# Psum copies of the w2-transpose products and of the last output products fixed to ScalarE, and three n3 stores moved to ScalarE's queue

## The chip, the cores and the metric

The kernel runs on one core of a Trainium2 chip, as one program. A core has TensorE (PE), VectorE (DVE), ScalarE (ACT), GpSimd (POOL) and SyncE (SP), each with its own instruction queue that is worked off in order, and they meet by semaphores. The metric is the device time of one execution in microseconds; the number given is the median of several runs.

## The reference

One block of a spectral transformer with adaptive norms, forward and backward, in bf16, with S = 2048 tokens, D = 1024 channels and F = 3584 hidden channels:

```python
mod = (_silu(c) @ w_mod).reshape(c.shape[0], 6, 1, -1)   # sa, ca, ga, sb, cb, gb
h = _layernorm(x) * (1 + ca) + sa
x = x + ga * A(h)          # A: rfft2 over (S, D), times w_r + 1j*w_i, irfft2
h = _layernorm(x) * (1 + cb) + sb
x = x + gb * B(h)          # B: layernorm, gelu(y @ w1 + b1) @ w2 + b2
...
out, vjp = jax.vjp(f, A_x, A_w_r, A_w_i, B_w1, B_b1, B_w2, B_b2, c, w_mod)
return (out, *vjp(grad_out))
```

The outputs are the forward result and the gradients of nine inputs. n3 below is the output of the third layer norm, the input of w1.

## The kernel before, in words

The program goes through five stages. First come the modulation rows and the first norm. The forward spectral mixer follows, with the 2D transform as matrix products: `spectral_core(True, ...)`, up to about 390 us. Beside its end PE computes the products "ph" = w2 transposed times the gated output gradient, and the stage ends in the z blocks, which make z = w1 n3 and the gelu with its derivative, interleaved with `bo_pass`, the second MLP product and the forward output (to about 500 us). The backward products through w1 follow, then the backward mixer with the norms' backward passes, beside which the gradients of w2 and of w1 are made as a list of pieces that fill PE.

Work on an engine stands in the order in which the tile scheduler put it when the program was built. `tc.high_priority()` and `tc.issue_after(...)` steer it; `nc.any` leaves it to the scheduler which of DVE and ACT does a copy.

The parts that the change and the prediction touch:

- **ph_part** (L832 to L847). For each of 28 blocks of 128 hidden channels and each of four quarters of the tokens, 8 matmuls of 128x512 (L839) fill a psum tile `pp`, of which there are four. A copy by `nc.any` (L845) puts it into `pho` or `phr` in SBUF; after the fourth quarter POOL stores the block to `d_ph`.
- **consume_fwd** (L884 to L904). For each quarter i of the tokens the inverse transform's output products `po` (L774, copies L779 and L781) are unfolded by additions on DVE (helper line L195), the result is stored by POOL (`d_A`), x is added, and two norms are applied. Statistics come from DVE (L493, L494, L503) and, for some rows, from ACT (L507, L510); the square root is ACT's L483; ACT applies the norm (L518). For the last quarter DVE applies the third norm. Line L904 stores n3 from SP to `d_n3`, 1024 KB at a time. The buffer from which it is stored (`ct`) is needed again for the unfolding of a later quarter. The two norms of a quarter go through the same scratch tile `mv`.
- **SP's queue** around there also holds the DMA transposes that load w2 transposed (L342 into `wt`), w1 and the reloads of `d_ph`. A store of n3 stands in line with these.
- **z_block** (L961 to L1002). For each group of four blocks: four products (L976), four ACT passes with the bias (L979), square (L983), two sigmoids (L987, L989), and on DVE L984, L990 and products (L195). `gt` are its tiles, `hhA`, `hhB`, `hhC` its results. In `bo_pass` PE sums the gradient of gb (L1049), and DVE brings the sum from psum to SBUF (L1052).
- **Backward**: `consume_bwd` (from L1474) unfolds, loads x again, applies the norm on ACT (L518) after the copy that is kept in `last_po`, multiplies, and calls the norm's backward (L1250, L1256, L1259). The pieces of the gradient of w1 run beside it: 16 matmuls (L1565) into a psum tile `gw1acc`, a copy by ACT (L1569) and a store. Psum tiles of `po` come from the same set as those of `gw1acc` for one copy in four.

Of the kernel before, what the change touches and what calls it, by code (L numbers as in the profile page):

```python
# [35 lines left out]
def kernel(  # L36
# [24 lines left out]
    nc = tc.nc  # L61
# [47 lines left out]
    d_n3 = dram.tile([S, D], BF16, name="d_n3")  # L109
# [16 lines left out]
    def chunk_rows(dt, i):  # L126
        return dt[4 * i * P:4 * (i + 1) * P, :].rearrange("(q p) d -> p q d", p=P)
# [400 lines left out]
    last_po = [None]  # L528
# [19 lines left out]
    def spectral_core(fwd, fb, sms, em, css, pt, evac_u, evac_c, evac_v, consume, o4tag, pfs=None, fill=lambda n: None, mid=lambda: None, beside=lambda n, r_in: None):  # L548
# [156 lines left out]
        for par in range(2):  # L705
            for m in range(4):
# [14 lines left out]
                if par == 0 and m > 0:  # L721
# [6 lines left out]
                    else:  # L728
                        cl = (CE, SE)[m - 2]
                        for h in range(2):  # L730
                            with tc.issue_after((ld_in if fwd else hh_in)[0].ins):
                                nc.sync.dma_start_transpose(out=gm[:, 2 * cl:2 * cl + 2, h * P:(h + 1) * P],
                                                            in_=d_E[:, v, 2 * cl + h, :])
# [22 lines left out]
        for i in range(4):  # L756
# [7 lines left out]
            for npp, (cl, ov4, c0) in enumerate((half if i % 2 == 0 else []) + [(cl, o4[:, cl], i * P) for cl in (CO, SO)]):  # L764
                if npp in (2, 4) and (fwd or (i, npp) != (0, 2)):
                    fill(1)
                for hh_ in range(2):
                    npo[0] += 1
                    po = ((ps_d, ps_s) if fwd else (ps_d, ps_s, ps_d, ps_f))[npo[0] % (2 if fwd else 4)]("po")
                    for d2 in range(2):  # L770
                        dc = 2 * hh_ + d2
                        for h in range(2):
                            gi = 2 * dc + h + (4 if (dc >= 2 and cl >= 2) else 0)
                            nc.tensor.matmul(po[:, d2 * 256:(d2 + 1) * 256], lhsT=Vs[cl][:, 2 * dc + h, c0:c0 + P],  # L774
                                             rhs=gm[:, gi, :], start=(h == 0), stop=(h == 1))
                    with tc.high_priority():
                        ov = ov4[:, hh_ * 512:(hh_ + 1) * 512]
                        if fwd or (cl, hh_) != (3, 0):
                            nc.any.tensor_copy(out=ov, in_=po[:])  # L779
                        else:  # L780
                            last_po[0] = nc.scalar.copy(out=ov, in_=po[:])  # L781
            if i % 2 == 0:
                tt(o4[:, 0:4:2, :], eb[:, 0:2, :], eb[:, 2:4, :], ALU.add)
                if fwd and i == 2:
# [49 lines left out]
    def ph_part(fc, js):  # L834
        ph2 = phs[fc % 4]
        for j in js:
# [5 lines left out]
            ov = ph2[:, :, q * P:(q + 1) * P]  # L842
            pv = pp[:, :].rearrange("p (i w) -> p i w", w=P)
            with tc.high_priority():
                nc.any.tensor_copy(out=ov, in_=pv)  # L845
        if js[-1] == 3:
            nc.gpsimd.dma_start(out=d_ph[fc * P:(fc + 1) * P, :], in_=ph2.rearrange("p i w -> p (i w)"))  # L847

# [35 lines left out]
    def consume_fwd(i, o4, tmp, tmp2, x4, eb):  # L884
# [14 lines left out]
        else:  # L899
            for q in range(4):  # L900
                t = 4 * i + q
                nc.vector.tensor_scalar(out=tmp[:, q, :], in0=tmp[:, q, :], scalar1=stats[:, 2, 0, t:t + 1],
                                        scalar2=stats[:, 2, 1, t:t + 1], op0=ALU.mult, op1=ALU.add)
        nc.sync.dma_start(out=chunk_rows(d_n3, i), in_=tmp)  # L904

    spectral_core(True, fbuf, (smA, smB), em1[:, 1], [css[:, 0], css[:, 1]], new_pair_temps(PXT[2:6]),
                  act_copy, act_copy, act_copy, consume_fwd, "fr")
# [789 lines left out]
```

## Time and profile before

| what | before |
|---|---|
| median of 3 runs | 1398.17 us (1397.17 to 1399.39) |
| profiled execution | 1398.61 us |
| its span, first to last instruction | 1396.8 us |
| busy share of PE / DVE / ACT / POOL | 97% / 76% / 55% / 25% |
| mean granted TensorE clock | 0.990 |
| copies of `pp` by ACT / DVE | 77 / 35 |
| copies of `po` by ACT / DVE | 43 / 21 |

The times that one reads in the trace are of the profiled execution, and start at its first instruction. Rows of the timeline give start, duration, engine, line, operation, output and inputs, the number of equal instructions in a row, and in brackets how long the engine stood idle before and what ended that. Rows that belong together overlap a little at their ends, so several in a row take less than their durations' sum. A windows row gives, for one stretch of time, the busy time of each engine (with the number of instructions), the granted clock of TensorE, the share of the DMA engines and GB/s. A DMA's time from issue to landing stands last in the rows on DMA issues.

### The profile page before, as it was taken

The numbers are of one execution on the slowest core, as the hardware profiler recorded it, in microseconds if no ns is written. First come the engines' busy times: TensorE is split into PE (matmuls) and PEld (weight loads), VectorE is DVE, ScalarE is ACT, GpSimd is POOL, SyncE is SP. The second block draws the span as 40 slices with busy tenths as digits, with TensorE's granted clock in tenths as the row PEclk, the third lists the DMA queues.
The fourth block names the chain that finished last, engine by engine and source line by source line (L and its number), as shares of the span: only waits on it lengthen the run. The fifth ranks groups of instructions, "written<-read, shape, count | busy, mean of one in ns | idle before, by whom it ended". The sixth has DMA issues, their size and how long they took to land.

```text
span 1396.8 us, 18464 instructions
## 1 busy us (share of the span) xinstructions
PE 1351.6 (97%) x6774; PEld 657.6 (47%) x6899; DVE 1063.7 (76%) x1471; ACT 767.6 (55%) x1090; POOL 347.8 (25%) x434
## 2 busy tenths in 40 slices
PE   4998999999999999999999999999999999999998
PEld 2545566444444444444444444444654555444444
DVE  4997889977888787787811388889888489976990
ACT  4875657657977766656503684445732454534311
POOL 5410533301212122122111011011444320332351
PEclk8999999999999999999999999999999999999999
DMA  9982755899787777697999979988679978899991
GB/s 318 289 237 57 202 143 189 259 273 357 241 246 247 229 248 239 202 275 247 244 319 219 220 185 272 306 275 231 216 221 259 222 205 200 218 232 239 292 344 64
DMA packets 360689, 331.12 MB, mean 237 GB/s; under 512 B 207962, under 2 KB 303088, under 8 KB 360470
## 3 DMA queue, kind: packets, MB, share of 16 engines
q1 hardware_dynamic: 319702, 204.96, 56.9%
q0 software_dynamic: 35136, 119.73, 25.0%
q10 hardware_dynamic: 5760, 5.25, 1.2%
q8 instruction: 54, 0.88, 0.3%
q14 instruction: 37, 0.30, 0.1%
HBM read 165.73 MB, written 114.87 MB: 201 GB/s over the span
## 4 chain that ended last, share of the span: by engine, by line
PE 72%; DVE 7%; DMA 3%; issue 1%; ACT 1%; ACTq 0%; DVEq 0%
PE pg L1130 14%; PE gw1acc L1565 13%; PE gw2acc L1302 13%; PE pz L976 13%; PE pbo L1030 13%; DVE ct L195 4%; PE pp L839 2%; PE po L774 1%; DVE st L493 1%; PE pcs L581 1%; DMA hhsA<-d_hh 1%; DMA w2sA<-in_B_w_dram 1%; DMA d_n<-ct 1%; PE acc3a L218 1%; PE pu L542 1%
## 5 line engine op out<-in xcount | busy, mean ns | idle before, releaser
L839 PE MATMUL pp<-gBoT,wt 128*128 128x512 bf16 x874 | 197.9, 383 | 4.1 <-ACT phr L845 2.9
L1130 PE MATMUL pg<-w1T,gzr 128*128 128x512 bf16 x877 | 194.3, 379 | 1.3 <-issue 0.5
L1565 PE MATMUL gw1acc<-gzh,n3n 128*128 128x512 bf16 x626 | 139.1, 379 | 3.6 <-DVE ct L779 2.8
L839 PEld LDWEIGHTS <-wt 128*128 128x128 bf16 x896 | 88.0, 98 | 108.2 <-issue 7.3
L1565 PEld LDWEIGHTS <-n3n 128*128 128x128 bf16 x896 | 87.4, 98 | 108.2 <-issue 4.4
L1130 PEld LDWEIGHTS <-gzr 128*128 128x128 bf16 x896 | 86.6, 98 | 108.4 <-issue 5.8
L976 PEld LDWEIGHTS <-w 128*128 128x128 bf16 x896 | 87.3, 98 | 106.8 <-issue 2.4
L976 PE MATMUL pz<-n3Tb,w 128*128 128x512 bf16 x437 | 98.4, 379 | 1.6 <-DVE w2sD L1052 0.9
L976 PE MATMUL pz<-n3Ta,w 128*128 128x512 bf16 x439 | 98.0, 379 | 0.4
L195 DVE TENSOR_TENSOR ct<-ct 128x2048 bf16<-128x2048 bf16 (+1 forms) x84 | 91.6, 1119 | 7.1 <-DMA d_n<-ct 4.7
L1030 PEld LDWEIGHTS <-hhA 128*128 128x128 bf16 x608 | 58.9, 98 | 72.7 <-issue 2.5
L1302 PE MATMUL gw2acc<-gB,hhsA 128*128 128x512 bf16 x405 | 91.7, 379 | 0.6
L1569 ACT CAST gwo<-gw1acc 128x512 bf16<-128x512 f32 x56 | 32.2, 581 | 108.3 <-PE gw1acc L1565 87.8
L979 ACT ACTIVATE gt<-pz,b_col 128x512 bf16<-128x512 f32 x112 | 72.9, 682 | 33.3 <-PE pz L976 33.0
L987 ACT ACTIVATE gt<-gt 128x2048 bf16<-128x2048 bf16 x28 | 53.5, 1911 | 64.3 <-DVE gt L195 64.3
L195 DVE TENSOR_TENSOR gt<-gt,gt 128x2048 bf16<-128x2048 bf16 x56 | 68.6, 1224 | 19.8 <-ACT gt L989 18.5
L1310 ACT CAST gwo<-gw2acc 128x512 bf16<-128x512 f32 x40 | 23.6, 590 | 85.8 <-PE gw2acc L1302 85.8
L1302 PEld LDWEIGHTS <-hhsA 128*128 128x128 bf16 x416 | 40.7, 98 | 47.2
L1565 PE MATMUL gw1acc<-gzu,n3n 128*128 128x512 bf16 x251 | 55.2, 379 | 0.3
L983 ACT ACTIVATE gt<-gt 128x2048 bf16<-128x2048 bf16 x28 | 53.5, 1909 | 2.3 <-DVE hhC L195 1.6
L989 ACT ACTIVATE gt<-gt 128x2048 bf16<-128x2048 bf16 x28 | 53.4, 1907 | 0.4
L1302 PE MATMUL gw2acc<-gB,otl 128*128 128x512 bf16 x218 | 49.2, 379 | 0.4 <-issue 0.2
(371 smaller groups left out, 2511.0 us busy)
## 6 DMA issues: line engine op xcount, KB each, us to landing
gzr<-d_gz SPq DMA_DIRECT2D x28, 512.0 KB
wblk<-in_w_mod_dram SPq DMA_DIRECT2D x12, 1024.0 KB
d_ph<-pho POOLq DMA_DIRECT2D x21, 512.0 KB, 5.6
out_dram<-otl POOLq DMA_DIRECT2D x40, 256.0 KB, 4.8
d_hh<-hhA POOLq DMA_DIRECT2D x19, 512.0 KB, 5.0
wrw<-in_w_mod_dram SPq DMA_DIRECT2D x32, 256.0 KB
w<-in_B_w_dram SPq DMA_DIRECT2D x7, 1024.0 KB
hhC<-d_ph SPq DMA_DIRECT2D x14, 512.0 KB
```

What stands on the lines that cost most here:

```text
L195: return nc.vector.tensor_tensor(out=out, in0=a, in1=b, op=op)
L839: last_pe[0] = nc.tensor.matmul(pp[:], lhsT=wt[:, fc % 4, cch, :], rhs=gBoT[j][:, cch, :], start=(cch == 0), stop=(cch == NDC - 1))
L976: last_pe[0] = nc.tensor.matmul(pz[:], lhsT=w1s[g][:, cch, k * P:(k + 1) * P], rhs=n3T[:, cch, :], start=(cch == 0), stop=(cch == NDC - 1))
L979: z_in = nc.scalar.activation(out=zb[:, k, :], in_=pz[:], func=ACT.Identity, bias=b1_col[:, fc:fc + 1], scale=1.0)
L983: nc.scalar.activation(out=av, in_=zb, func=ACT.Square)
L987: nc.scalar.activation(out=sg, in_=bv, func=ACT.Sigmoid, scale=2.0 * GK)
L989: nc.scalar.activation(out=bv, in_=bv, func=ACT.Sigmoid, scale=-2.0 * GK)
L1030: last_pe[0] = nc.tensor.matmul(pbs[i][:], lhsT=hh[:, k, i * P:(i + 1) * P], rhs=wp[:, k, :], start=False, stop=(g == 6 and k == 3))
L1130: last_pg[0] = nc.tensor.matmul(pgs[i][:], lhsT=gzs[b, g][:, k, i * P:(i + 1) * P], rhs=w1Ts[g][:, k, h * KH:(h + 1) * KH], start=(g == 0 ...
L1302: nc.tensor.matmul(acc[:], lhsT=hh_of(fc)[:, t, :], rhs=gBs[t // 4][:, t % 4, h * KH:(h + 1) * KH], start=(t == 0), stop=(t == NT - 1))
L1565: nc.tensor.matmul(acc[:], lhsT=n3ns[t // 4][:, t % 4, cch * P:(cch + 1) * P], rhs=gz2[t // 8][:, t % 8, :], start=(t == 0), stop=(t == NT ...
L1569: w1g["ev"] = nc.scalar.copy(out=ob, in_=acc[:])
```

## The change

```diff
@@ spectral_core
                         ov = ov4[:, hh_ * 512:(hh_ + 1) * 512]
-                        if fwd or (cl, hh_) != (3, 0):
+                        if not fwd and (i == 3 or (cl, hh_) == (3, 0)):
+                            last_po[0] = nc.scalar.copy(out=ov, in_=po[:])
+                        else:
                             nc.any.tensor_copy(out=ov, in_=po[:])
-                        else:
-                            last_po[0] = nc.scalar.copy(out=ov, in_=po[:])
@@ ph_part
             with tc.high_priority():
-                nc.any.tensor_copy(out=ov, in_=pv)
+                (s_copy if fc >= 13 else act_copy)(ov, pv)
@@ consume_fwd
-        nc.sync.dma_start(out=chunk_rows(d_n3, i), in_=tmp)
+        (nc.scalar if i < 3 else nc.sync).dma_start(out=chunk_rows(d_n3, i), in_=tmp)
```

`s_copy` is `nc.scalar.copy` and `act_copy` is `nc.any.tensor_copy`. So all copies of `pp` from the fourteenth block on are ACT's; those before stay free. In the backward mixer all copies of the last quarter are ACT's, and the norm there waits for the last of them. Three of four n3 stores are issued by ACT, the last by SP as before. In the program as built 22 copies of `pp` move from DVE to ACT (99 / 13 now) and one of `po` (44 / 20). PE's order stays as it was. DVE's and ACT's orders are made anew by the scheduler. Copies through the two helpers show their lines, L803 and L806, in place of L845.

ACT around the norm statistics of the third quarter, before; `pp` copies into `pho` and `phr`, the square root (L483), the norm's rows (L518):

```order
L845 CAST pho<-pp 128x4x128 x5
L845 CAST phr<-pp 128x4x128 x3
L483 ACTIVATE mv<-mv,eps_c 128x4
L845 CAST phr<-pp 128x4x128
L845 CAST pho<-pp 128x4x128
L518 ACTIVATE ct<-ct,stats 128x1024 x2
```

The same place in the changed program:

```order
L806 CAST pho<-pp 128x4x128 x3
L806 CAST phr<-pp 128x4x128 x4
L806 CAST pho<-pp 128x4x128
L483 ACTIVATE mv<-mv,eps_c 128x4
L806 CAST pho<-pp 128x4x128 x3
L507 ACTIVATE ct,mv<-xt 128x1024
L518 ACTIVATE ct<-ct,stats 128x1024
```

The square root stands two copies later, behind all four copies into `phr`, and one row of the next statistics has come in behind it. On DVE the statistics themselves (L493) for that square root, before:

```order
L195 TENSOR_TENSOR ct<-ct 128x4x512 x2
L195 TENSOR_TENSOR ct<-ct,rows_86 128x4096
L195 TENSOR_TENSOR ct<-ct 128x8x256
L195 TENSOR_TENSOR ct<-ct,sb_saf 128x4096
L195 TENSOR_TENSOR ct<-ct 128x4x2x256
L493 BN_STATS st<-ct 128x6 x3
```

And in the changed program, with the same first rows (these are what waits for the n3 store's buffer):

```order
L195 TENSOR_TENSOR ct<-ct 128x4x512 x2
L195 TENSOR_TENSOR ct<-ct 128x8x256
L195 TENSOR_TENSOR ct<-ct 128x4x2x256
L195 TENSOR_TENSOR ct<-ct 128x2x1024
L195 TENSOR_TENSOR ct<-ct,rows_86 128x4096
L195 TENSOR_TENSOR ct<-ct 128x2x1024
L195 TENSOR_TENSOR ct<-ct,sb_saf 128x4096
L195 TENSOR_TENSOR ct<-ct 128x2x1024
L493 BN_STATS st<-ct 128x6 x3
```

Three more rows of the next quarter's unfolding stand ahead of the statistics.

ACT where the last quarter's second norm meets the first z block, before; `gt_3066` is the tile of z block 0:

```order
L483 ACTIVATE mv<-mv,eps_c 128x4
L518 ACTIVATE ct<-xt,stats 128x1024
L979 ACTIVATE gt_3066<-pz,b_col 128x512
L518 ACTIVATE ct<-xt,stats 128x1024
L979 ACTIVATE gt_3066<-pz,b_col 128x512
L518 ACTIVATE ct<-xt,stats 128x1024
L979 ACTIVATE gt_3066<-pz,b_col 128x512
L518 ACTIVATE ct<-xt,stats 128x1024
L979 ACTIVATE gt_3066<-pz,b_col 128x512
L983 ACTIVATE gt_3066<-gt_3066 128x2048
```

The changed program, from the store of n3 (third quarter) on:

```order
L904 DMA d_n_98<-ct 128x4x1024
L979 ACTIVATE gt_3066<-pz,b_col 128x512 x2
L507 ACTIVATE ct,mv<-xt 128x1024
...
L979 ACTIVATE gt_3066<-pz,b_col 128x512
L510 ACTIVATE ct,mv<-xt,mv 128x1024
L806 CAST pho<-pp 128x4x128
L483 ACTIVATE mv<-mv,eps_c 128x4
L983 ACTIVATE gt_3066<-gt_3066 128x2048
L806 CAST pho<-pp 128x4x128
L518 ACTIVATE ct<-xt,stats 128x1024
L806 CAST pho<-pp 128x4x128
L518 ACTIVATE ct<-xt,stats 128x1024
```

The four L979 and the square L983 of z block 0 now stand ahead of the four L518, which have copies between them.

ACT near the end of the backward mixer, the piece of the difference (L779 and L781 are the copies of `po`, L1569 those of the gradient of w1):

```order
-L779 CAST ct<-po 128x512 x2
-L781 CAST ct<-po 128x512
-L518 ACTIVATE xt<-xt,stats 128x1024 x4
-L1569 CAST gwo_9633<-gw1acc 128x512 x6
+L779 CAST ct<-po 128x512 x4
+L518 ACTIVATE xt<-xt,stats 128x1024 x3
+L1569 CAST gwo_9633<-gw1acc 128x512
+L518 ACTIVATE xt<-xt,stats 128x1024
+L1569 CAST gwo_9633<-gw1acc 128x512 x5
```

The fourth copy of the last quarter, which DVE did between a multiplication with a loaded tile and the fold behind it, now stands on ACT ahead of the norm, and one copy of the gradient of w1 has moved into the norm's rows.

## Prediction

> **What bounds the kernel now.** I read the page's busy times first, then the chain that ended last, then what TensorE (PE) waits for.
>
> ```profile
> PE 1351.6 (97%) x6774; PEld 657.6 (47%) x6899; DVE 1063.7 (76%) x1471; ACT 767.6 (55%) x1090; POOL 347.8 (25%) x434
> ...
> PE 72%; DVE 7%; DMA 3%; issue 1%; ACT 1%; ACTq 0%; DVEq 0%
> ```
>
> PE is busy for 97% of the span and makes up 72% of the chain. The other engines count only where PE waits for them. Of its waits, those of 0.9 us or more after 130 us are these three (earlier ones lie ahead of all that the change touches):
>
> ```profile
> PE pp L839 <- ACT phr L845: 2.9, 1, 2.9
> PE gw1acc L1565 <- DVE ct L779: 2.8, 1, 2.8
> PE pz L976 <- DVE w2sD L1052: 0.9, 1, 0.9
> ```
>
> Columns: total us, times, longest. The first two end with copies of the kind that the change moves. So I take each apart, and ask what PE meets next.
>
> **The wait at 316.73.** Rows of the timeline of PE, ACT, DVE and SP around it (start, us, engine, line, and in brackets the idle time ahead and what ended it):
>
> ```profile
> 299.88 13.97 PE L839 MATMUL pp<-gBoT,wt 128*128 128x512 bf16 x63
> 316.73 10.48 PE L839 MATMUL pp<-gBoT,wt 128*128 128x512 bf16 x39 [2.87 <-ACT phr L845]
> ...
> 315.90 0.30 ACT L483 ACTIVATE mv<-mv,eps_c 128x4 f32<-128x4 f32 x1 [8.33 <-DVE mv L494]
> ...
> 300.62 2.36 DVE L195 TENSOR_TENSOR ct<-ct 128x2048 bf16<-128x2048 bf16 x2 [4.73 <-DMA d_n<-ct]
> ...
> 291.51 0.40 SPq L904 DMA_DIRECT2D d_n<-ct  x1
> ```
>
> PE stopped at 299.88 + 13.97 = 313.85 with its four psum buffers full. Their copies stood on ACT behind the square root L483, which waited 8.33 us for the norm's statistics on DVE. DVE was late because it resumed only at 300.62, when the store of n3 (second quarter, issued on SP at 291.51) had landed and its buffer was free: 9.1 us from issue to landing. Two edits touch this: copies go to ACT, and the store leaves SP.
>
> The wait also costs clock:
>
> ```profile
> 120.77 1.46 PE L542 MATMUL pu<-smA,fbuf 128*128 128x256 bf16 x6 [3.97 <-DVE fbuf L195]
> ...
> 120.00:140.00 20.00, 18.87 (x119) 12.93 (x121) 11.48 (x17) 13.30 (x22) 0.00 (x0) 0.84 0.14 20
> ...
> 310.00:320.00 10.00, 7.13 (x28) 2.89 (x27) 9.96 (x20) 2.86 (x5) 0.80 (x2) 0.89 0.99 295
> 320.00:330.00 10.00, 9.95 (x44) 4.46 (x44) 8.71 (x13) 8.72 (x13) 1.26 (x2) 0.94 1.03 366
> ...
> 1270.00:1280.00 10.00, 7.12 (x33) 3.20 (x33) 4.91 (x4) 1.28 (x3) 2.14 (x2) 1.00 1.21 255
> ```
>
> The third number from the end is the granted clock. Behind this wait it is 0.89 and 0.94 in two windows of 10 us: 0.11 x 10 + 0.06 x 10 = 1.7 us lost. Behind the 3.97-us wait of L542 it is 0.84 over 20 us, about 3 us. Behind the wait near 1278 it is 1.00: nothing. At stake at 316 are 2.87 + 1.7 = 4.6 us.
>
> The clock rule of the Trainium skill ("TensorE: Matmul & The Clock Gate", Part 1: The HAM clock gate) is that PE falls to half clock after an idle window of about 3.4 us, a window that runs freely. The 2.87-us wait lost clock though it is shorter, and that near 1278 did not, so the rows decide here; by the page the 4.7-us wait found below would surely lose some.
>
> **What replaces it.** I walked each engine's new row order with the durations above and below.
>
> ```profile
> 299.27 2.01 ACT L845 CAST pho<-pp 128x512 bf16<-128x512 f32 x4
> ...
> 286.99 1.88 DVE L845 CAST pho<-pp 128x512 bf16<-128x512 f32 x3
> ...
> 286.85 4.63 ACT L518 ACTIVATE ct<-ct,stats 128x1024 bf16<-128x1024 bf16 x4 [0.65 <-DVE stats L195]
> ...
> 324.60 1.06 ACT L507 ACTIVATE ct<-xt 128x1024 bf16<-128x1024 bf16 x1 [0.62 <-DVE xt L195]
> ...
> 329.07 1.13 ACT L510 ACTIVATE ct<-xt,mv 128x1024 bf16<-128x1024 bf16 x1
> ...
> 338.36 1.91 ACT L983 ACTIVATE gt<-gt 128x2048 bf16<-128x2048 bf16 x1
> ...
> 353.37 2.40 ACT L979 ACTIVATE gt<-pz,b_col 128x512 bf16<-128x512 f32 x4
> ...
> L1311 ACTq DMA_DIRECT2D out_dram<-gwo x40: 338/338/374, 1018.5 to 1188.4; - x40
> ```
>
> A copy takes 0.50 us on ACT (2.01 / 4) and 0.60 on DVE (1.88 / 3). 22 of the 112 move, so ACT gains 11 us and DVE is rid of 13, nearly all beside busy PE. An L518 takes 4.63 / 4 = 1.16 on ACT (1.13 from start to start, as rows overlap by 0.1 at their ends; so I count L983 as 1.8), an L979 0.6. Issuing a store takes ACT 0.34 us (the row's ns, on its weight-gradient stores) to the 0.40 that SP shows, three times.
>
> 1. *The second n3 store.* Before, its four norm rows (L518) start at 286.85. After, copies and one L507 no longer stand ahead of the statistics and they start at about 284.2 by walking; 4 x 1.13, and three copies of 0.5 among them, give an issue at 290.2, 1.3 us earlier than on SP. The landing after the issue, L, isn't shown for ACT's queue. Bounds:
>
> ```profile
> d_A<-ct POOLq DMA_DIRECT2D x4, 1024.0 KB, 5.7
> ```
>
> From 5.7 (the same 1024 KB, on POOL's queue) to 9.1 (its own landing on SP). I take 7.4, the middle: its size speaks for the first row, its moment, with the DMA engines as full as they were, for the second. DVE resumes at 297.6, 3.0 earlier.
>
> 2. *The statistics.* The new DVE order puts three more unfold rows ahead of the statistics of this quarter (half of the 2.36-us pair at 300.62 each, 1.13 to 1.18, with gaps 3.8 in all). So L483 runs at 315.9 - 3.0 + 3.8 = 316.7: no earlier. But on ACT two more psum tiles are copied ahead of L483. PE does a tile of 8 matmuls in 1.7 us (an L1565 group of 16, below, takes 3.5: 16 x 17.43 / 79), so it runs out not at 313.85 but at 317.3, and meets a free buffer at 316.7 + 0.2 + 0.5 = 317.4. **The wait at 316 goes**, up to some tenths.
>
> 3. *What is late next.* PE is now nearly 3 us ahead (4.6 with the clock). It needs DVE and ACT next in the z blocks (L961 to L1002), and there stands the 0.94-us wait of the list:
>
> ```profile
> 337.79 2.29 DVE L195 TENSOR_TENSOR ct<-ct,rows 128x4096 bf16<-128x4096 bf16 x1 [6.42 <-ACT ct L518]
> ...
> 353.50 1.22 DVE L195 TENSOR_TENSOR gt<-gt,gt 128x2048 bf16<-128x2048 bf16 x1 [0.72 <-ACT gt L989]
> ...
> 360.40 0.69 DVE L990 TENSOR_SCALAR gt<-gt 128x2048 bf16<-128x2048 bf16 x1
> 362.34 1.22 DVE L195 TENSOR_TENSOR hhB<-gt,gt 128x2048 bf16<-128x2048 bf16 x1 [1.25 <-ACT gt L987]
> ...
> 447.85 0.69 DVE L1052 COPY w2sD<-pa 128x512 f32<-128x512 f32 x1
> ...
> 448.59 1.89 PE L976 MATMUL pz<-n3Tb,w 128*128 128x512 bf16 x8 [0.94 <-DVE w2sD L1052]
> ...
> 337.79:447.85 110.06, 109.23 (x505) 49.15 (x514) 96.55 (x103) 85.33 (x80) 22.36 (x27) 1.00 0.83 256
> ```
>
> From 337.79 on, where the last quarter's norm releases it, DVE works almost without a break (96.55 of 110.06, the rest handed to and fro with ACT) until L1052 at 447.85, for which PE waits. **That chain, not PE, sets when PE passes 448.** A gain of PE ahead of it is waited away there, unless the chain moves too.
>
> Does it? After, ACT issues the third n3 store, then does z block 0's four L979, the statistics' L507 and two L510, L483, L983 and two copies ahead of the four L518 of the last quarter; before, those L518 came first. From L483 at 316.7: L507 and the four L518 of the third quarter with four copies end at 328.9 by walking (their inputs come from DVE at 321.3), then 0.4 + 4 x 0.59 + 1.06 + 2 x 1.13 + 2 x 0.5 + 0.2 + 1.8 = 9.1, then 4 x 1.13 + 3 x 0.5 = 6.0. DVE's row of 337.79 starts at about 344.1, **6.3 us later**. To make up for it, rows of z block 0 (L984, a multiply, L990: 0.6 + 1.13 + 0.6) and three copies (1.8) no longer lie between it and the row at 362.34: 4.1 us; and of the two waits for ACT there (0.72 and 1.25) some 1.6 go, since z block 0 is through sooner. 6.3 - 5.7 = 0.6. **The wall moves 0.6 us later** with L = 7.4, and one for one with L: -1.1 for 5.7, +2.3 for 9.1. So the 4.6 us are taken back whole: PE stands still for about 4.7 us at 448 instead of 2.87 at 316 and 0.94.
>
> 4. *Clock behind the wall.* A stop of 4.7 us in one piece is longer than both that lost clock, 1.7 and 3.0 us above, and one of 2.83 lost none. Bounds 0 and 3.0; I take 2.0, nearer to the row next to it in time.
>
> The Trainium skill ("DMA: Bandwidth & Descriptors", Issuing engines are not separate DMA queues) says that transfers started on different engines run on the same 16 DMA engines, so that a start elsewhere saves only the starting engine's time; that would leave L near 9.1 and speaks against edit three. The same page (Queues, rings and completion order) has each DMA engine take turns between its queue rows, which would let the store pass SP's transposes; with a DMA share of 0.99 no row of before tells the two apart.
>
> **The wait at 1277.93.** Here one copy (L779) goes to ACT.
>
> ```profile
> 1274.98 2.29 DVE L195 TENSOR_TENSOR ct<-ct,xt 128x4096 bf16<-128x4096 bf16 x1 [11.62 <-DMA xt<-d_gx]
> 1277.19 0.68 DVE L779 CAST ct<-po 128x512 bf16<-128x512 f32 x1
> ...
> 1277.93 17.43 PE L1565 MATMUL gw1acc<-gzh,n3n 128*128 128x512 bf16 x79 [2.83 <-DVE ct L779]
> ...
> 1297.20 3.52 ACT L1259 ACTIVATE ct<-xt,s1c,sc 128x1024 bf16<-128x1024 bf16 x3 [8.09 <-DVE s1c L1250]
> 1300.63 0.56 ACT L1569 CAST gwo<-gw1acc 128x512 bf16<-128x512 f32 x1
> ...
> 1303.18 7.07 PE L1565 MATMUL gw1acc<-gzh,n3n 128*128 128x512 bf16 x31
> 1310.09 10.09 PE L1565 MATMUL gw1acc<-gzu,n3n 128*128 128x512 bf16 x45
> ...
> 1314.09 1.06 ACT L1645 ACTIVATE sr<-accSA 1x512 f32<-1x512 f32 x2 [9.58 <-DVE ct L195]
> 1315.06 1.51 ACT L1569 CAST gwo<-gw1acc 128x512 bf16<-128x512 f32 x3
> ```
>
> The copy stood on DVE behind a row that waited 11.62 us for a load. On ACT it runs at about 1265.5, ahead of L518: PE no longer waits, 2.83 us. What is late next: DVE's chain starts at 1274.98 whatever PE does, and is shorter only by the copy (0.7 us). So ACT's copies behind L1259 and L1645 come at 1300.63 - 0.7 + 0.57 = 1300.5 and 1315.06 - 0.7 + 0.57 = 1314.9, while PE, 2.8 us earlier, wants their psum buffers at about 1300.4 (its group of 1303.18) and 1314.2 (two groups of 3.5 after that of 1310.09). Waits of about 0.2 and 0.7 come back: the gain is 2.83 - 0.9, or **1.8** with the gaps. Bounds: 1.3, if the chain starts no earlier, and 2.8.
>
> **Sum.** 1398.61 (profiled execution; its span is 1396.8) + 0.6 (wall) + 2.0 (clock) - 1.8 = 1399.4. The median before, 1398.17, lies 0.44 lower: **1399.0**.
>
> **Rivals.**
> - *Both waits go for good*: the DVE chain moves along with PE. -2.87 - 1.7 - 2.83 = -7.4, 1390.8. For it: ACT is busy for 55% only and DVE loses 13 us of copies. Against: step 3, where the last norm stands behind z block 0. 0.12.
> - *The store lands fast*: L = 5.7, wall -1.1, no clock lost, -1.8: -2.9, 1395.3. For it: one queue to itself. 0.19.
> - *Slower than before, by the late last norm*: L of 9.1 or more puts the wall 2.3 later, the clock costs 1.9 to 3.0 and the end returns only 1.3: +2.9 to +4.0, 1401.1 to 1402.2. It decides from L = 8.5 (+1.7 wall, 2.5 clock, -1.4: +2.8). For it: DMA shares of 0.99 and 1.03 (the number behind the clock) in the windows above. Against: the 5.7 of the store of equal size. 0.26.
> - *ACT can't keep up*: 15 blocks in a row have all copies on one engine, behind four L518 (4.63 us); with four psum tiles of 1.7 us PE has 6.9 us of slack, and each L518 group now has copies between. If they get stuck for 3 us twice, +6, 1404. 0.07.
> - *Nothing changes*, as the free choice picked these engines already: only 22 and one copies move, but the row order shows that they do and that the store leaves SP. No chance of its own.
>
> **How the numbers follow.** The forecast (0.36) is 1399.0. All bounds low: 1398.2 - 1.1 - 2.8 = 1394.3; all high: 1398.2 + 2.3 + 3.0 - 1.3 = 1402.2. With a run's spread of 1 us, 1393.3 to 1403.3 leaves out the first rival and half of the fourth. A measurement can tell about 0.2%, 2.8 us: faster takes the first rival and half of the second, 0.24; slower the third mostly, the fourth, and a margin, 0.34; same 0.42.
>
> **What would show it.** Right: no wait of PE near 316; DVE's row of 337.79 near 344; one wait of 4 to 5 us at L1052 near 448, and a granted clock below 1.00 in the window behind it; no wait at 1278 but small ones at 1300 and 1314. Wrong: a wait at L1052 below 2 us (the chain moved along), a store that lands in under 6 or over 9 us, or new waits of PE for ACT's copies between 290 and 350.

## The result and the profile after

The changed kernel takes 1411.47 us (median of 4 runs, 1406.52 to 1417.6), the kernel before beside it 1397.67: a ratio of 1.0100, with a 95% interval of 1.0074 to 1.0127. It is slower by 1.0%, where no measurable change was forecast. The profiled execution took 1408.52 us, with a span of 1406.7, 9.9 us more than that of before.

The page of the changed kernel first, then its list of what PE waits for (those of 0.5 us or more for another engine or a DMA after 130 us; "..." stands for earlier ones):

```profile
PE 1352.8 (96%) x6774; PEld 657.3 (47%) x6899; DVE 1054.0 (75%) x1448; ACT 778.6 (55%) x1113; POOL 345.6 (25%) x434
```

```profile
PE pp L839 <- ACT pho L806: 5.7, 1, 5.7
PE pu L1445 <- ACT smbf L806: 4.1, 1, 4.1
...
PE pz L976 <- DVE w2sD L1052: 2.3, 1, 2.3
PE gw2acc L1302 <- ACT gwoE L1313: 1.9, 1, 1.9
PE pp L839 <- DMA wt<-in_B_w_dram: 1.8, 1, 1.8
...
PE pbo L1030 <- DMA w2sA<-in_B_w_dram: 1.5, 1, 1.5
...
PE gw1acc L1565 <- ACT gwo L1569: 0.5, 1, 0.5
```

The copies did move: DVE has 9.7 us less work and ACT 11.0 more. PE's own work is the same within 1.2 us. So nearly all that was lost is waiting. Of 0.9 us or more before had three, after has six, and the largest is in the place from which the prediction took one away. The timeline there, on PE, ACT, DVE and SP:

```profile
315.94 1.90 PE L839 MATMUL pp<-gBoT,wt 128*128 128x512 bf16 x8 [1.76 <-DMA wt<-in_B_w_dram]
323.58 6.77 PE L839 MATMUL pp<-gBoT,wt 128*128 128x512 bf16 x23 [5.74 <-ACT pho L806]
...
453.06 1.89 PE L976 MATMUL pz<-n3Tb,w 128*128 128x512 bf16 x8 [2.27 <-DVE w2sD L1052]
...
288.73 0.38 ACTq L904 DMA_DIRECT2D d_n<-ct  x1
...
322.76 0.30 ACT L483 ACTIVATE mv<-mv,eps_c 128x4 f32<-128x4 f32 x1 [13.13 <-DVE mv L494]
...
303.82 6.01 DVE L195 TENSOR_TENSOR ct<-ct 128x2048 bf16<-128x2048 bf16 x5 [12.58 <-DMA d_n<-ct]
...
349.62 2.29 DVE L195 TENSOR_TENSOR ct<-ct,rows 128x4096 bf16<-128x4096 bf16 x1 [3.71 <-ACT ct L518]
...
452.32 0.68 DVE L1052 COPY w2sD<-pa 128x512 f32<-128x512 f32 x1
...
281.17 12.28 SPq L961 DMA_TRANSPOSE n3Ta<-d_n  x1
293.54 3.42 SPq L342 DMA_TRANSPOSE wt<-in_B_w_dram  x1
297.15 0.44 SPq L918 DMA_DIRECT2D w<-in_B_w_dram  x1
297.68 7.37 SPq L342 DMA_TRANSPOSE wt<-in_B_w_dram  x1
```

Read it from the store. ACT issues it at 288.73, 2.8 us earlier than SP did. But DVE, whose unfold waits for its buffer, resumes only at 303.82: the store took **15.1 us** from issue to landing, 9.1 before. All behind it is late: the square root L483 (322.76, before 315.90), hence the copies of `pho` and `phr`, hence PE's 5.74 us, and the last norm on DVE (349.62, before 337.79).

SP's rows tell what the store ran beside. The transpose of n3 for the first z block (L961) takes SP 12.28 us, and more transposes of w2 and a load of w1 (L918) follow. Windows rows of after, with the DMA share and GB/s at the end:

```profile
280.00:300.00 20.00, 19.89 (x93) 9.04 (x94) 3.35 (x13) 17.69 (x26) 1.60 (x3) 1.00 1.25 183
...
320.00:330.00 10.00, 6.36 (x23) 2.58 (x24) 9.97 (x17) 4.39 (x8) 1.53 (x2) 0.83 1.09 362
...
450.00:460.00 10.00, 7.68 (x36) 3.44 (x36) 8.56 (x8) 7.39 (x7) 3.79 (x4) 1.00 0.82 265
```

and the first of them in the profile of before:

```profile
280.00:300.00 20.00, 19.85 (x91) 9.00 (x92) 11.23 (x26) 15.33 (x21) 1.83 (x3) 1.00 0.97 246
```

From 280 to 300 the DMA engines are more taken up (share 1.25 for 0.97) and move less (183 GB/s for 246). DVE works 3.35 us of 20, before 11.23.

The trace's record of DMA packets tells more. Its rows name a queue, the number of packets, MB and the share of the 16 DMA engines' time. q1 is SP's queue, q0 POOL's, and q10 ACT's (5.25 MB in the whole program before and 8.39 after, which is three n3 stores more). From 288 to 296, behind the store's issue, in the changed kernel:

```profile
q1 hardware_dynamic: 2808, 0.72, 122.1%
q0 software_dynamic: 108, 0.39, 13.9%
```

and from 296 to 304:

```profile
q10 hardware_dynamic: 528, 1.05, 37.7%
q1 hardware_dynamic: 1949, 0.53, 35.0%
q0 software_dynamic: 288, 1.05, 32.5%
```

Not one packet of the store moved in the first stretch, and all 528 in the second, from 296.98 to 303.30. So more than half of the 15.1 us is a standstill of 8.3 us, while SP's queue moved mostly small packets (2820 of the 2917 of all queues in that stretch are under 512 bytes). The first n3 store of the same program, issued by ACT at 261.85, had its first packet after 1.0 us and its last landed at 265.92.

How much later PE starts the same group than in the first profile of before, in us: -1.2 at 192 (ahead of all that the change touches, a difference that executions of one program have), +3.2 at 327, +4.5 behind the wall at 448, +5.1 at 708, +7.2 at 990, +12.3 at 1166 and +9.9 behind the last mixer at 1295. So the store's stage lost 5.7, and later places 7.8, of which 2.4 came back.

### The profile page after: what moved, and what is told of

It reads as the page before. It is cut to its first block, busy times and chain, and to the rows that moved or that the text cites. A ratio compares the mean times of both kernels' runs of the same rounds, so it can differ in the third digit from the quotient of the medians.

```text
span 1406.7 us, 18462 instructions
## 1 busy us (share of the span) xinstructions
PE 1352.8 (96%) x6774; PEld 657.3 (47%) x6899; DVE 1054.0 (75%) x1448; ACT 778.6 (55%) x1113; POOL 345.6 (25%) x434
## 3 DMA queue, kind: packets, MB, share of 16 engines
q10 hardware_dynamic: 7344, 8.39, 1.8%
## 5 line engine op out<-in xcount | busy, mean ns | idle before, releaser
L979 ACT ACTIVATE gt<-pz,b_col 128x512 bf16<-128x512 f32 x112 | 73.2, 684 | 34.6 <-PE pz L976 34.4
L1569 ACT CAST gwo<-gw1acc 128x512 bf16<-128x512 f32 x56 | 32.3, 584 | 100.8 <-PE gw1acc L1565 86.8
L983 ACT ACTIVATE gt<-gt 128x2048 bf16<-128x2048 bf16 x28 | 53.5, 1911 | 1.8 <-DVE hhC L195 1.0
```

The lines of the kernel that those rows point to most:

```text
L979: z_in = nc.scalar.activation(out=zb[:, k, :], in_=pz[:], func=ACT.Identity, bias=b1_col[:, fc:fc + 1], scale=1.0)
L983: nc.scalar.activation(out=av, in_=zb, func=ACT.Square)
L1569: w1g["ev"] = nc.scalar.copy(out=ob, in_=acc[:])
```

## The experiments

**Theory A**: edit three makes the loss. The store, started by ACT while SP goes on issuing transposes and loads, lands far later than in line on SP. **Theory B**: the copies do it (edit two, or one), by holding up ACT. **Theory C**: the new row order does it, with the last norm behind z block 0, whatever the store takes. "L" is the store's time from issue to DVE's row that waits for it. "Wall" is how much later PE is behind L1052 than in the first profile of before, in brackets with the difference at 192 taken off. A profile of the kernel before shows what one program varies by: in a second one the wall is at -1.4 (-0.3).

### The edits apart

`e1_po` has only the copies of `po`, `e2_pp` only those of `pp`, `e3_store` only the stores, `e12_no_store` the first two:

```diff
 e1_po and e12_no_store
-                        if fwd or (cl, hh_) != (3, 0):
+                        if not fwd and (i == 3 or (cl, hh_) == (3, 0)):
 e2_pp and e12_no_store
-                nc.any.tensor_copy(out=ov, in_=pv)
+                (s_copy if fc >= 13 else act_copy)(ov, pv)
 e3_store
-        nc.sync.dma_start(out=chunk_rows(d_n3, i), in_=tmp)
+        (nc.scalar if i < 3 else nc.sync).dma_start(out=chunk_rows(d_n3, i), in_=tmp)
```

> Only the first edit: the output products' copies of the last backward quarter fixed to ScalarE. Both theories expect the same of the forward part, as it is not touched. Near the end TensorE's wait of 2.83 us for DVE's copy (L779) should be gone and at most some 0.9 us should come back behind L1569: 1.3 to 2.8 us faster than before. If the end is bound by the loads of the norm's backward instead, no difference.

> Only the second edit: copies of the w2-transpose products from the 14th block on by ScalarE. Theory 'store' (the loss comes from the n3 store on ScalarE's queue, which took 15.1 us from issue to landing instead of 9.1): the store stays on SP and lands in 8 to 10 us, DVE resumes near 300, the time is within 2.8 us of before. Rival 'copies' (the loss comes from the row order that the copies bring, three more unfold rows ahead of the statistics, and L483 later): 6 to 10 us slower than before, TensorE waits 4 us or more for a copy near 320.

> Only the third edit: three n3 stores issued by ScalarE. Theory 'store': the second one lands 13 us or more after its issue, SP's transpose of n3 (L961) takes over 10 us, and the time is 5 to 10 us above before. Rival 'copies': the store lands in about 9 us, time within 2.8 us of before.

> First and second edit, all n3 stores on SP as before. Theory 'store': 0 to 4 us faster than before, since the end's gain stays and the store is out of the way of the transposes. Rival 'copies': still 4 to 8 us slower than before.

| kernel | median us | ratio to before (95%) | L | L961 on SP | wall |
|---|---|---|---|---|---|
| e1_po | 1394.73 | 0.9981 (0.9964 to 0.9998) | 8.3 | | -1.1 (-0.8) |
| e2_pp | 1395.84 | 0.9985 (0.9961 to 1.0008) | 5.0 | 4.5 | -4.3 (-3.0) |
| e3_store | 1402.78 | 1.0033 (1.0017 to 1.0048) | 9.1 | 10.5 | +1.7 (+3.2) |
| e12_no_store | 1397.91 | 1.0011 (0.9991 to 1.0031) | 5.2 | 4.2 | -5.4 (-2.9) |

Only the kernel with the stores is slower, so the copies alone are not the loss, and B falls. `e3_store` has a third of the loss that the whole change first showed, and about that of its later measurement (0.39%, below). But its second store lands in 9.1 us as in the kernel before, where 13 or more were expected: its loss is not a late landing. In its profile, of the slowest of its ten executions, one more unfold row stands ahead of the statistics (16.55 us from DVE's resume to L483, before 15.28), PE waits 3.16 and 1.60 us near 320, and behind a stop of 2.26 us at the wall the clock is 0.93 and 0.90 in two windows of 10 us, 1.7 us lost. Rows of `e12_no_store`:

```profile
287.37 0.39 SPq L904 DMA_DIRECT2D d_n<-ct  x1
287.85 3.20 SPq L342 DMA_TRANSPOSE wt<-in_B_w_dram  x1
291.22 0.45 SPq L918 DMA_DIRECT2D w<-in_B_w_dram  x1
...
292.56 2.36 DVE L195 TENSOR_TENSOR ct<-ct 128x2048 bf16<-128x2048 bf16 x2 [4.63 <-DMA d_n<-ct]
...
329.53 2.29 DVE L195 TENSOR_TENSOR ct<-ct,rows 128x4096 bf16<-128x4096 bf16 x1 [6.24 <-ACT ct L518]
...
442.44 0.68 DVE L1052 COPY w2sD<-pa 128x512 f32<-128x512 f32 x1
...
982.48 9.43 PE L1302 MATMUL gw2acc<-gB,hht 128*128 128x512 bf16 x32 [5.11 <-ACT gwoE L1313]
```

The load of w1 stands behind the store and a transpose on SP, the store lands in 5.2 us, the last norm's row comes at 329.53, 8.3 earlier than before, and the wall moves along to 442.44: the first rival of the prediction, for these two edits. Then PE waits 5.11 us at 982 and the gain is gone (below, "the late place").

### Where the stores are issued

`x_pool` puts the three stores on POOL's queue, `x_first` and `x_second` only one of them on ACT's, all in the otherwise changed kernel:

```diff
-        (nc.scalar if i < 3 else nc.sync).dma_start(...)
+        (nc.gpsimd if i < 3 else nc.sync).dma_start(...)     x_pool
+        (nc.scalar if i == 0 else nc.sync).dma_start(...)    x_first
+        (nc.scalar if i == 1 else nc.sync).dma_start(...)    x_second
```

> The whole change, but the three n3 stores issued by GpSimd and not by ScalarE. Theory 'transposes': GpSimd's queue isn't SP's either, SP runs on with transposes, and the second store takes 9 us or more; 5 to 14 us slower than before. Rival 'queue': it lands in 4 to 7 us as GpSimd's other stores of 1024 KB do, and the time is within 3 us of before.

> First and second edit, and only the first quarter's n3 store on ScalarE; the second is on SP again. Theory 'transposes', with the second store as the one that DVE waits for: SP holds its transposes back at the second store, which lands in 5 to 7 us; time within 3 us of before. Rival 'backlog' (the first store already sets SP's transposes back, and n3's transpose L961 takes 10 us or more whatever the second store does): L961 stays above 9 us, the second store gets out late, 4 us or more slower than before.

> First and second edit, and only the second quarter's n3 store on ScalarE. Theory 'transposes': this store alone makes most of the loss: it lands after 9 us or more, 5 to 14 us slower than before. Rival 'backlog': with the first store on SP the transposes are not behind, L961 takes 4 to 6 us, the second store lands in 7 us or less, and the time is within 3 us of before.

| kernel | median us | ratio to before (95%) | L | L961 on SP | wall |
|---|---|---|---|---|---|
| x_pool | 1398.47 | 1.0001 (0.9986 to 1.0017) | 10.2 | 5.8 | +3.2 (+3.2) |
| x_first | 1399.01 | 1.0013 (0.9994 to 1.0032) | 8.5 (SP) | 7.8 | +0.2 (-0.8) |
| x_second | 1399.01 | 1.0010 (0.9992 to 1.0027) | 12.3 | 4.2 | +5.4 (+4.5) |

Rows of `x_second`:

```profile
283.12 4.20 SPq L961 DMA_TRANSPOSE n3Ta<-d_n  x1
...
290.80 0.43 ACTq L904 DMA_DIRECT2D d_n<-ct  x1
...
303.06 6.01 DVE L195 TENSOR_TENSOR ct<-ct 128x2048 bf16<-128x2048 bf16 x5 [11.69 <-DMA d_n<-ct]
```

With the second store alone on ACT it lands late (12.3) and the wall moves, though L961 takes 4.20 us as on SP: a long L961 is not needed for a late store. SP issues a load of w1 there 0.7 us ahead of the store (290.11), where in the kernel before it comes 0.6 behind. The long L961 came only with the first store on ACT. In the same kernels POOL also issues a 512-KB store of `d_ph` 0.2 to 0.7 us behind L961's start (at 281.68 in after), in the others no store before 1.3 us; the runs don't tell these two apart.

None of the three variants loses measurably, though by theory 'transposes' `x_pool` and `x_second` should have lost 5 us or more, and their stores do land late (10.2 and 12.3). So no single one of the first two stores makes a loss of 0.9%, and it is not enough that all three leave SP; a loss of 0.2 to 0.3% the intervals don't exclude. Of the kernels so far only those with all three on ACT are slower. The third store was not moved alone; neither PE nor DVE nor ACT waits for it in the profile of after.

### What the store runs beside

In these kernels SP's neighbours of the store are taken away, in the changed kernel. `y_hold` issues the first two loads of w1 later; `x_plain` makes the transposing loads near the store plain ones, and so leaves that transposition out:

```diff
 y_hold and y_hold_plain
-            load_w1({24: 1, 25: 1, 27: 5}.get(fc, 0))
+            load_w1({27: 7}.get(fc, 0))
 x_plain and y_hold_plain, w2 blocks from the fifteenth on (n3 of the first z block alike)
-        w2t_in[0] = nc.sync.dma_start_transpose(out=wt[:, fc % 4], in_=...)
+        w2t_in[0] = nc.sync.dma_start(out=wt[:, fc % 4], in_=...)
```

> The whole change, with the transposing loads next to the second n3 store (w2 blocks from the 14th on, and n3's first transpose) made plain loads of the same bytes, so ph and the first z blocks are computed from untransposed data; every engine's row order stays. Theory 'transposes' (the store is slow on ScalarE's queue because SP no longer holds its transposes back while the store runs): the second store lands in 4 to 7 us, DVE resumes before 296, TensorE's waits near 316 and 323 are below 1 us, and the time is 5 to 15 us below the changed kernel, at 1393 to 1402. Rival 'queue' (ScalarE's queue is slow by itself): it still takes 9 us or more and DVE resumes after 298.

> The whole change, but SP issues the first two loads of w1 (1024 KB each, L918) only behind the last w2 transpose and not beside the second n3 store. Theory 'transposes': the store still takes 11 us or more, since n3's and w2's transposes still run beside it, and the time is within 4 us of the changed kernel's. Rival 'any load' (what counts is the bytes that SP has in flight beside the store, the w1 load most of all): the store lands in 9 us or less, DVE resumes before 299, TensorE's wait near 323 falls below 3 us, 3 us or more faster than the changed kernel.

> Both: the first two w1 loads held back, and the transposing loads beside the store made plain loads (ph and the first z blocks come from untransposed data). Little is in flight beside the store. Both theories: it lands in 4 to 6 us. If ScalarE's queue is slow by itself, it still takes 9 us or more.

The changed kernel itself was profiled again, five times in all, to see what one execution is worth:

> The changed kernel once more, beside the others, with a second profile. The second store should again land 12 us or more after its issue and TensorE wait 4 us or more near 320; the two waits of the first profile near 990 (1.9 us) and 1162 (4.1 us) should come back if they belong to the change, and be another size if they are a race between GpSimd's or ScalarE's stores and SP's transposes. Time 1404 to 1414.

> The changed kernel, third profile. Theory 'forward': TensorE passes 448 between 5 and 8 us later than in the kernel before in every execution, as the second n3 store lands 12 us or more after its issue; what differs between executions are waits near 990 and 1160 of 0 to 8 us in sum. Rival: the spread comes from the landing of the n3 store itself, which goes over 18 us in the slowest executions.

> The changed kernel, fourth profile, one execution. As for the third: 5 to 8 us late at the wall of 448 by theory 'forward', and what varies are the waits near 990 and 1160; by the rival the n3 store's landing varies.

> The changed kernel, fifth profile, one execution. As for the third: 5 to 8 us late at the wall of 448 by theory 'forward', and what varies are the waits near 990 and 1160; by the rival the n3 store's landing varies.

| store on ACT beside | L, us | of it until the store's first packet | first to last packet | profiles |
|---|---|---|---|---|
| transposes and a load of w1 (the changed kernel) | 15.1, 15.8, 15.2, 22.0, 16.3 | 8.3, 9.1, 6.1, 5.0, 5.7 | 6.3, 6.3, 7.7, 16.6, 10.1 | after, after_again, after_p1, after_p2, after_p3 |
| transposes, no load of w1 | 10.2 | 4.9 | 4.5 | y_hold |
| a load of w1, plain loads for the transposes | 8.4 | 3.1 | 4.7 | x_plain |
| no load of w1, plain loads for the transposes | 4.6 | 0.9 | 3.2 | y_hold_plain |

Rows of `x_plain` (its lines 907, 921, 982 and 1058 are 904, 918, 976 and 1052 of the others):

```profile
288.56 0.53 SPq L921 DMA_DIRECT2D w<-in_B_w_dram  x1
...
290.15 0.39 ACTq L907 DMA_DIRECT2D d_n<-ct  x1
...
298.53 6.01 DVE L195 TENSOR_TENSOR ct<-ct 128x2048 bf16<-128x2048 bf16 x5 [5.83 <-DMA d_n<-ct]
...
344.30 2.29 DVE L195 TENSOR_TENSOR ct<-ct,rows 128x4096 bf16<-128x4096 bf16 x1 [3.70 <-ACT ct L521]
...
447.75 3.47 PE L982 MATMUL pz<-n3Tb,w 128*128 128x512 bf16 x8 [3.41 <-DVE w2sD L1058]
```

of `y_hold`:

```profile
288.33 0.38 ACTq L904 DMA_DIRECT2D d_n<-ct  x1
...
298.56 6.02 DVE L195 TENSOR_TENSOR ct<-ct 128x2048 bf16<-128x2048 bf16 x5 [7.69 <-DMA d_n<-ct]
```

of `y_hold_plain`:

```profile
288.58 0.38 ACTq L907 DMA_DIRECT2D d_n<-ct  x1
...
293.15 6.01 DVE L195 TENSOR_TENSOR ct<-ct 128x2048 bf16<-128x2048 bf16 x5 [2.03 <-DMA d_n<-ct]
...
446.83 2.54 PE L982 MATMUL pz<-n3Tb,w 128*128 128x512 bf16 x8 [3.51 <-DVE w2sD L1058]
```

and of `after_p2`, the slowest landing:

```profile
281.73 13.57 SPq L961 DMA_TRANSPOSE n3Ta<-d_n  x1
...
301.59 14.09 SPq L342 DMA_TRANSPOSE wt<-in_B_w_dram  x1
...
288.95 0.39 ACTq L904 DMA_DIRECT2D d_n<-ct  x1
...
310.90 6.02 DVE L195 TENSOR_TENSOR ct<-ct 128x2048 bf16<-128x2048 bf16 x5 [19.43 <-DMA d_n<-ct]
```

ACT's queue is not slow by itself: beside plain loads of w2 and n3 alone, the 1024 KB land in 4.6 us. Transposes in their place add 5.6 (10.2 - 4.6), the load of w1 3.8 (8.4 - 4.6), both together 10.5 and more. That part of A is shown, with one profile for each of the three emptied cells; that of `y_hold` is of its fastest execution (1396.91, the median is 1405.17). Both middle cells lie between what the theories had expected of them (11 or more against 9 or less, 4 to 7 against 9 or more).

But shorter landings did not bring the time back. `x_plain` takes 1403.16 us, 1.0039 (1.0015 to 1.0064), where 1393 to 1402 were expected; `y_hold` 1405.17, 1.0059 (1.0033 to 1.0084); beside `y_hold` the changed kernel itself (`after_again`) takes 1402.28, 1.0039 (1.0020 to 1.0059). `y_hold_plain` took 1399.79 in one execution.

What the store does to the wall can be read from the rows. With the changed order and the three stores on ACT (the five profiles of the changed kernel, these three, and `f_after` of the next section) L483 runs 18.9 us behind DVE's resume and the last norm's row 26.8 to 26.9 behind that; in the kernel before it is 15.3 and 21.9. From that row to L1052 it is 102.7 us (before 110.1) in all but `y_hold_plain`. In sum that is 148.5 us for 147.2: the new order by itself costs 1.3 us at the wall, and what the store is late moves it one for one. So C is right only for 1.3 us, and the rest of the wall's shift comes from the late resume. In `y_hold_plain` DVE resumes 7.5 us earlier than before, but waits 4.30 us at 380.80 for the last n3 store, which the held loads of w1 now run beside, so that 102.7 becomes 107.2.

That a gain of PE is taken back at the wall shows in both kernels with plain loads: in `x_plain` PE is 3.8 us ahead at 327 (start taken off) and waits 3.41 us there, `y_hold_plain` is 4.9 ahead and waits 3.51, and behind each stop the clock costs 1.7 us more (0.88 and 0.95, 0.90 and 0.93 in windows of 10 us). So even the fastest landing only reaches a wall at -0.07 (+1.2).

### The late place, and the program against itself

Near 980 ACT's scaling L1602 waits for POOL's small stores of its results, which run beside SP's transpose L1523, and PE waits behind ACT. In the first profile of after:

```profile
988.08 2.19 ACT L1602 ACTIVATE gw<-gr,u_rt 128x1024 bf16<-128x1024 bf16 x2 [7.98 <-DMA out_dram<-gw]
...
980.47 9.66 SPq L1523 DMA_TRANSPOSE hht<-d_hh  x1
```

and in that of before:

```profile
979.23 2.19 ACT L1602 ACTIVATE gw<-gr,u_rt 128x1024 bf16<-128x1024 bf16 x2 [4.12 <-DMA out_dram<-gw]
...
976.28 5.51 SPq L1523 DMA_TRANSPOSE hht<-d_hh  x1
```

The same transpose takes 9.66 us for 5.51 and the stores twice as long. PE lost 2.1 us there in after, 7.6 in `e12_no_store`, 4.1 in `after_again`, 2.6 in `after_p1`, and nothing in `after_p2` and `after_p3`: it goes one way or the other in different executions of the same program. To take this place out, the results get a second tile:

```diff
+    gw5b = reg.tile([P, 4, D], BF16, name="gw5b", tag="uv3")
+    gw5s = [gw5[:, k, :] for k in range(4)] + [gw5b[:, k, :] for k in range(4)]
-            nc.scalar.activation(out=gw5[:, jc % 4, :], ...)
+            nc.scalar.activation(out=gw5s[jc], ...)
```

This is in the kernel before (`f_before`), in the changed one (`f_after`) and in that without the stores (`f_e12`); `before_again` is the kernel before, unchanged.

> The kernel before once more, for a second profile. The waits of 2.87 us at 316 and 0.94 at 448 should come back within half a microsecond. The wait of 2.83 at 1278 hangs on a load's landing: in the kernels without the first edit and with the copy still on DVE it was under 0.3, so it may be anything from 0 to 4 us.

> The kernel before, with eight buffers and not four for the rows of the last modulation gradient (L1602), so that ScalarE no longer waits for their stores near 980. If that wait only shows in some executions of the kernel before: 0 to 3 us faster than before, and no wait of TensorE over 0.5 us near 985.

> The changed kernel with the same eight buffers. Theory 'forward' (the loss is the late second n3 store alone): 4 to 8 us slower than f_before, with the store landing 12 us or more after its issue and no wait near 985. Rival 'late stage' (the change also makes later stages slower): more than 8 us slower than f_before, or waits elsewhere.

> First and second edit with the same eight buffers, all n3 stores on SP. If the 2.9 us that the copies gain at 448 were given back only by the wait near 980: 2 to 5 us faster than f_before and the fastest kernel of all. Rival: another wait takes its place and it is within 1.5 us of f_before.

| kernel | median us | ratio to before (95%) |
|---|---|---|
| f_before | 1396.79 | 0.9997 (0.9976 to 1.0017) |
| f_after | 1410.08 | 1.0088 (1.0064 to 1.0112) |
| f_e12 | 1393.97 | 0.9981 (0.9962 to 0.9999) |

In none of the three profiles does PE wait near 985. The changed kernel is still 0.88% slower, so the late place is not the cause of the loss; its profile has L = 15.5, waits of 1.02 and 6.79 near 320 and the wall at +7.5. By the medians it is 13.3 us slower than `f_before`, more than the 4 to 8 of theory 'forward', which speaks for the rival 'late stage'. Its profile, of the fastest of its six executions (1402.93), shows no later loss: +7.5 still at 1005.

The kernel without the stores, freed of that place, is 0.19% faster than before, as `e1_po` is, though both intervals end just below 1. Its profile, of one of its slower executions (1397.49), doesn't have the gain at the wall: the store lands in 5.1 us and the last norm is early, but DVE waits 1.97 us for the last n3 store at 383.73, PE stops for 2.99 us, and the wall is at +2.4 (+0.3).

`before_again` took 1393.69 us in its one execution, and shows that a wait that the prediction counted on is not always there:

```profile
1269.80 2.29 DVE L195 TENSOR_TENSOR ct<-ct,xt 128x4096 bf16<-128x4096 bf16 x1 [9.03 <-DMA xt<-d_gx]
...
1262.67 27.79 PE L1565 MATMUL gw1acc<-gzh,n3n 128*128 128x512 bf16 x126
```

PE goes through in one row of 126 matmuls: DVE's row behind the load came 5.2 us earlier than in the first profile, where PE was only 1.9 ahead, and the 2.83-us wait at 1278 is absent, as it is in `e2_pp` and `e3_store`, which leave that copy as it was.

The profiles of the changed program side by side (PE later than in the first profile of before, us):

| profile | time | L | waits of PE at 310 to 331 | at 192 | behind the wall | at 1005 | at 1393 |
|---|---|---|---|---|---|---|---|
| after | 1408.52 | 15.1 | 1.76 + 5.74 | -1.2 | +4.5 | +7.2 | +9.9 |
| after_again | 1404.22 | 15.8 | 1.29 + 6.88 | -2.0 | +4.4 | +7.6 | +5.6 |
| after_p1 | 1403.72 | 15.2 | 2.77 + 4.50 | +0.5 | +6.3 | +8.0 | +5.1 |
| after_p2 | 1407.15 | 22.0 | 6.32 + 1.10 + 0.23 + 4.89 | -1.0 | +13.2 | +12.4 | +8.6 |
| after_p3 | 1406.58 | 16.3 | 0.79 + 4.49 + 1.51 | -0.5 | +9.2 | +9.6 | +8.0 |

Between 192 and the wall the five lose 5.7, 6.4, 5.8, 14.2 and 9.7 us, 8.4 in the mean; `before_again` gained 0.3 there. That stage is the loss that all of them share, and it is the one that holds the store.

## Why the prediction was wrong, point by point

The forecast for the profiled execution was 1399.4, and it came to 1408.52, 9.1 more. By the terms of the sum: wall +4.5 instead of +0.6 (+3.9); clock behind the wall 0 instead of 2.0 (-2.0); the end -2.4 instead of -1.8 (-0.6); and three places that had no term, 0.65 at 708, 2.05 at 990 and 5.1 from 1106 to 1166 (mostly PE's 4.1 us for ACT's copy `smbf`, which none of the other profiles of this program has).

1. **The second n3 store: the step that failed.** The term is L. The issue was to come at 290.2 and came at 288.73. The landing was to take 5.7 to 9.1 us, by the middle 7.4, and took 15.1 to 22.0. The bounds came from two stores of the same size with other surroundings: one on POOL's queue at another time, one on SP. What the sum left out is the company. In line on SP the store was issued at 291.51, after the transpose of n3 (282.20 to 287.86) had left that queue; on ACT it was issued at 288.73, in the middle of it (281.17 to 293.45), and stood still until 296.98. The four cells above show that these neighbours make the time, 4.6 us without and 15 and more with them. It is not that SP issues its work earlier once the store is gone: L961 comes 1.0 us earlier, but the load of w1 at 297.15 for 292.07. The order around the store counts as well: the 8.8 to 9.1 us of the kernel before have the load of w1 directly behind the store, the 12.3 of `x_second` directly ahead of it, and the 5.0 to 5.2 of `e2_pp` and `e12_no_store` have a transpose between the two. What made the packets stand still was not tried by itself.

   The Trainium skill ("DMA: Bandwidth & Descriptors", Issuing engines are not separate DMA queues) states that a start on another engine saves only that engine's issuing time, as the same 16 DMA engines carry all of it. That the move gains nothing agrees with the rows; that it costs is beyond it: L rose from 9.1 to 15.1. Nor did the turns between queues, which the prediction named, let the store pass: none of its packets moved from 288 to 296.

2. **The statistics.** L483 was to run at 316.7, and PE's wait at 316 to go. It ran at 322.76, and PE waits 1.76 and 5.74. The rule "resume of DVE plus a fixed path" held: 303.82 instead of 297.6 is 6.2 later, L483 6.1. That w2's transposes themselves would be late (1.76, in `after_p2` 6.32) was not thought of. The store is not what made L961 long: when it was issued, L961 had already taken 7.6 us (288.73 - 281.17), more than the 5.66 it takes in all before.

3. **What is late next.** DVE's row of the last norm was to start at 344.1 with L = 7.4, and one for one with L. With the issue 1.5 earlier and L 7.7 longer that gives 350.3; it came at 349.62. The wall was to move likewise, by 0.6 + 6.2 = 6.8; it moved 4.5, or 5.7 with the start taken off, as the path from DVE's resume to L1052 got 1.3 us longer and not 3.6. That a gain of PE is taken back at the wall was right: `x_plain` and `y_hold_plain`, in which PE comes early, wait 3.41 and 3.51 there. With the store on SP the order is another, and the norm is early (330.6 and 329.5 in `e2_pp` and `e12_no_store`): there the chain moves along, and PE's gain of 3.0 us stands as far as the late place. In `f_e12` it doesn't, for the last n3 store.

4. **Clock.** The stop of 2.27 us at the wall cost none: 1.00 from 450 to 460. That was luck of this execution. Stops of 2.10 (`after_p2`), 2.18 (`f_after`) and 2.26 (`e3_store`) at the same place lost 1.7 us each (0.83, 0.83, and 0.93 with 0.90, in windows of 10 us), one of 3.41 (`x_plain`) as much, and one of 3.38 (`after_p3`) 3.4 (0.70 and 0.96). So the term of 2.0 had a fair size, and the length of a stop alone doesn't tell what it costs. The stop of 5.74 near 320 cost 0.17 x 10 = 1.7 us (0.83). By the Trainium skill ("TensorE: Matmul & The Clock Gate", Part 1) half clock follows an idle window of about 3.4 us; the stops of 5.74 and 2.27 us agree with it, those of 2.10 to 2.26 do not.

5. **The wait at 1277.93.** It is gone, but a second profile of before does not have it either, so the change can't be given the credit. A term of 1.8 us rested on one execution. Against the first profile of before PE gains 2.1 to 3.0 us between 1166 and 1295 in every other profile, whether its kernel has the first edit or not. So the 0.19% of `e1_po` can't be put down to this wait.

The third rival named the direction and the mechanism (a landing of 8.5 us or more, a late last norm), at 1401.1 to 1402.2; its price ended at 9.1 us as the bound did. The fourth rival, copies stuck on ACT, is not what happened at 320: with the same copies and the stores on SP, PE waits at most 0.74 us there (`e12_no_store`).

What stays open: why the whole change costs 1.0% and 0.88% in two comparisons and 0.39% in a third, with its own kernel before beside it each time; the profiles show one stage whose loss varies from 5.7 to 14.2 us, but the slowest executions were not profiled. Why the wall's +3.2 and +5.4 in `x_pool` and `x_second` come out at a ratio near 1 is not settled either. It may be in part that single executions of the kernel before lie between 1392 and 1405 us and only two of them were profiled. What makes L961 long, and what decides how long L1523 takes, was not found.

## What to carry to other kernels

A transfer that stands in one queue with others is issued once they are through. On a free queue it may be issued in their midst, and then stand still behind them for longer than the line would have taken. Before moving it to a free queue, ask what will then run beside it, and look for the landing time of that very company rather than of the same size elsewhere. A wait that is to be counted as gain should be seen in more than one profile.

## What the runs showed of the hardware

- A store of 1024 KB from ACT's queue: 4.6 us beside plain loads of w2 and n3, 8.4 with a load of w1 as well, 10.2 beside DMA transposes, 15.1 to 22.0 beside transposes and a load of w1.
- Of the 15.1 us, 8.3 pass before the first packet moves, while SP's queue moves 2808 packets from 288 to 296 and POOL's 108.
- L961, the transpose of n3, took 4.2 to 5.8 us where the first store was not ACT's, 7.8 to 13.6 where it was and the transpose was kept.
- Over the 20 us around the store, the DMA engines' share rose from 0.97 to 1.25 while they moved 183 GB/s for 246: a higher share meant less moved.
- The transpose L1523 near 980 took 5.51 us in one profile, 9.66 in another and 12.45 in a third (`e12_no_store`); where it took 9.66, ACT waited 7.98 us for the small stores beside it, and 4.12 where it took 5.51.
- Stops of PE of 2.10 to 2.26 us cost 1.7 us of clock in three profiles, one of 2.27 nothing in a fourth.
